# Attention and a gated feed-forward layer on one core: a store moved to another queue, and an unused path rewritten

## The chip, the core and the metric

The kernel runs on one NeuronCore of a Trainium2 chip. The core has five engines with instruction streams of their own: TensorE (PE in the profile; its weight loads are PEld), VectorE (DVE), ScalarE (ACT), GpSimd (POOL) and SyncE (SP), which computes nothing and issues transfers. A name with a q (SPq, ACTq) is the part of an engine that takes instructions in order, waits on semaphores and issues transfers. Sixteen DMA engines carry the transfers of all queues. The metric is the device time of one execution in microseconds (us), as the median of several.

## The reference

Eight batches of eight heads attend causally over 576 positions, with a decay from a cumulative sum; the result, as 4608 rows of 512, is normalized and goes through a gated feed-forward layer with 1536 inner columns.

```python
scores = 0.125 * q @ k.T                       # per head, 576 x 576, head size 64
cum    = cumsum(maximum(s, 0))
bias   = minimum(-(cum[i] - cum[j]), 0)        # causal: j <= i
attn   = softmax(scores + bias) @ v            # -> x, 4608 x 512
xn     = x / sqrt(mean(x * x) + 1e-6) * rms_g
out    = (silu(xn @ w_gate) * (xn @ w_val)) @ w_out
```

The softmax is taken with its row maximum subtracted. Inputs and output are 32-bit floats.

## The kernel before

The kernel has two paths. The **fast path** holds nearly the whole program. It leaves out the row maximum and folds the decay into factors per key, which is right only while the sums of s and the sizes of q and k stay in bounds. It runs the feed-forward layer in nine chunks of 512 rows (`ffn(c)`). Attention work for the next rows is dealt out between the matmuls of a chunk by `step()`, which looks at lists of what is due (`s_seq`, `av_seq`, `xt_seq`, `t_seq`) and at lags in slots. For each of twelve blocks of 128 inner columns, TensorE makes the gate (L946) and the value (L955), ScalarE a tanh (L949), VectorE the products (L958, L951). At the end of a chunk `store` makes four tiles of 128 output rows: twelve matmuls each (L972), a copy with factor 0.5 by ScalarE into `osb` (L976), and a transfer to `out` (L977). The last tile of the last chunk is cut into columns 0 to 383 and 384 to 511, so that its last part is short.

While that runs, VectorE gathers what the bounds need into one number, `flag_i` (L1063). After the fast path `general` begins: every engine loads `flag_i` into a register (L1269) and branches on it (L1270). If it is 0, the **general path** computes everything again by the reference's rule. It has two loops that are run by registers. The first goes over the 64 heads (L1283): loads of k, q and v by GpSimd, the cumulative sum as a row and as columns from a copy in DRAM, TensorE transposes, scores, softmax, and 64-row pieces of the result into the DRAM buffer `x_d`. The second goes over 72 tiles of 64 rows (L1366): eight loads from `x_d`, the norm, a transpose, the feed-forward layer in three parts with a transpose each, and a store. With the inputs that are timed the flag is 1 and the branch goes past all of this.

What follows at L1270 on the side that skips is made by the framework, not written in the kernel: each engine raises the semaphores that its instructions in the general path would have raised, so that later waits hold on both sides. For SyncE these are the counters of its transfers, eight of them, each with a wait for the transfers so far. Then the program ends, at the line of the launch in the profile (L1432): SyncE waits for every semaphore in turn, two at a time, twelve waits; the engines meet in a barrier that GpSimd opens; GpSimd clears the semaphores; they meet again. The program's start (L1421) has a barrier of the same kind, ahead of which SyncE sets four registers and GpSimd three.

The order of all this on each engine is that in which the code is written or dealt out (`tc.manual_schedule()`). SyncE issues the stores of L977, the DMA transposes of the fast path (L190, L495) and, in the general path, all transfers but the loads of k, q and v.

Of the kernel before, what the change touches and what calls it, by code (L numbers as in the profile page):

```python
# [9 lines left out]
BF16 = mybir.dt.bfloat16  # L10
# [16 lines left out]
def kernel(  # L27
# [12 lines left out]
    nc = tc.nc  # L40
    B, H, S, D = q.shape
# [5 lines left out]
    NSC = 5  # L47
# [888 lines left out]
    def ffn(c):  # L936

        x0 = (c * DM) % RING
        first[0], chunk[0] = slot[0], c
        Ht = mp.tile([128, FB, DM], BF16, name="Ht", tag="Ht", bufs=2)  # L940
        pend = None
        for fb in range(FB):
            fs = slice(fb * 128, (fb + 1) * 128)
            Gp = psF()
            for cc in range(CC):
                nc.tensor.matmul(Gp, lhsT=wg_sb[:, cc, fs], rhs=xnT[:, cc, x0:x0 + DM],  # L946
                                 start=(cc == 0), stop=(cc == CC - 1))
            T = mp.tile([128, DM], FP32, name="T", tag="T", bufs=2)
            nc.scalar.activation(out=T, in_=Gp, func=AF.Tanh, scale=0.5)  # L949
            if pend is not None:  # L950
                nc.vector.tensor_tensor(out=Ht[:, fb - 1, :], in0=pend[0], in1=pend[1], op=ALU.mult)  # L951
            step(tanh=True)
            Vp = psF()
            for cc in range(CC):
                nc.tensor.matmul(Vp, lhsT=wv_sb[:, cc, fs], rhs=xnT[:, cc, x0:x0 + DM],  # L955
                                 start=(cc == 0), stop=(cc == CC - 1))
            U = mp.tile([128, DM], BF16, name="U", tag="U", bufs=2)
            nc.vector.scalar_tensor_tensor(out=U, in0=T, scalar=1.0, in1=Gp,  # L958
                                           op0=ALU.add, op1=ALU.mult)
            pend = (U, Vp)  # L960
            if fb < FB - 1:
                step()
        nc.vector.tensor_tensor(out=Ht[:, FB - 1, :], in0=pend[0], in1=pend[1], op=ALU.mult)
        step()
        def store(tb, parts):

            r0 = c * DM + tb * 128
            osb = mp.tile([128, DM], FP32, name="osb", tag="osb", bufs=3)
            for p0, p1 in parts:
                Op = psF()  # L970
                for fb in range(FB):
                    nc.tensor.matmul(Op[:, p0:p1], lhsT=Ht[:, fb, tb * 128:(tb + 1) * 128],  # L972
                                     rhs=wout_sb[:, fb, p0:p1], start=(fb == 0), stop=(fb == FB - 1))
                    if fb % 4 == 3 and fb < FB - 1 and p0 == 0:
                        step()
                nc.scalar.activation(out=osb[:, p0:p1], in_=Op[:, p0:p1], func=AF.Copy, scale=0.5)  # L976
                nc.sync.dma_start(out=out[r0:r0 + 128, p0:p1], in_=osb[:, p0:p1])  # L977
            step()

        for tb in range(4):  # L980
            store(tb, [(0, 384), (384, 512)] if c == NCH - 1 and tb == 3 else [(0, DM)])
# [279 lines left out]
def general(ctx, tc, q, k, v, out, wg_sb, wv_sb, wout_sb, g_row, cum, ident_bf, flag_i):  # L1261
# [8 lines left out]
    with tc.If(flag == 0, preferred_fallthrough_block=True):  # L1270
        with tc.tile_pool(name="gd", bufs=1, space=bass.MemoryType.DRAM) as gd, \
# [3 lines left out]
            x_d = gd.tile([9 * BH + 56, 64, D], FP32, name="x_d")  # L1275
            half = gs.tile([128, 1], FP32, name="half")
            nc.vector.memset(half, -0.5)
            nc.sync.dma_start(out=cum_d, in_=cum)
            qf = q.rearrange("b h s d -> (b h) s d")
            kf = k.rearrange("b h s d -> (b h) s d")  # L1280
            vf = v.rearrange("b h s d -> (b h) s d")
# [1 line left out]
            with tc.For_i(0, BH, 1) as i:  # L1283
# [9 lines left out]
                for w, src in ((0, kf), (1, qf)):  # L1293
# [5 lines left out]
                    "o (c p) d -> p (o c) d", p=128))  # L1299
                nc.gpsimd.dma_start(out=vn[0:64, 4, 0:D], in_=vf[one, 512:576, :].rearrange(  # L1300
                    "o p d -> p (o d)"))
                nc.sync.dma_start(out=crow, in_=cum_d[one, :].to_broadcast([128, S]))
                nc.sync.dma_start(out=ccol[:, 0:4], in_=cum_d[one, 0:512].rearrange(
                    "o (c p) -> p (o c)", p=128))
                nc.sync.dma_start(out=ccol[0:64, 4:5], in_=cum_d[one, 512:576].rearrange(
                    "o p -> p o"))
                kqt = gs.tile([D, 2, 640], BF16, name="kqt")
                for w in (0, 1):
# [6 lines left out]
                for qb in range(NSC):  # L1315
                    n = rows(qb)
                    nk = qb * 128 + n
                    sp = gp.tile([128, 1024], FP32, name="sp")
                    nc.tensor.matmul(sp[0:n, 0:min(nk, 512)], lhsT=kqt[:, 1, qb * 128:qb * 128 + n],
                                     rhs=kqt[:, 0, 0:min(nk, 512)], start=True, stop=True)  # L1320
                    if nk > 512:
                        nc.tensor.matmul(sp[0:n, 512:nk], lhsT=kqt[:, 1, qb * 128:qb * 128 + n],
                                         rhs=kqt[:, 0, 512:nk], start=True, stop=True)
                    sc = gs.tile([128, 640], FP32, name="sc")
                    nc.vector.tensor_scalar(out=sc[0:n, 0:nk], in0=crow[0:n, 0:nk],
                                            scalar1=ccol[0:n, qb:qb + 1], scalar2=0.0,
                                            op0=ALU.subtract, op1=ALU.min)
                    nc.vector.scalar_tensor_tensor(out=sc[0:n, 0:nk], in0=sp[0:n, 0:nk],
                                                   scalar=0.125, in1=sc[0:n, 0:nk],
                                                   op0=ALU.mult, op1=ALU.add)  # L1330
                    nc.gpsimd.affine_select(out=sc[0:n, qb * 128:nk], in_=sc[0:n, qb * 128:nk],
                                            pattern=[[-1, n]], compare_op=ALU.is_ge,
                                            fill=-1.0e30, base=0, channel_multiplier=1)
                    mx = gs.tile([128, 1], FP32, name="mx")
                    nc.vector.tensor_reduce(out=mx[0:n], in_=sc[0:n, 0:nk], axis=AX.X, op=ALU.max,
                                            negate=True)
                    pr = gs.tile([128, 640], BF16, name="pr")
                    nc.vector.memset(pr, 0.0)
                    nc.scalar.activation(out=pr[0:n, 0:nk], in_=sc[0:n, 0:nk], func=AF.Exp,
                                         bias=mx[0:n])  # L1340
                    pq = gp.tile([128, NSC, 128], BF16, name="pq")
                    for c in range(qb + 1):
                        nc.tensor.matmul(pq[:, c, :], lhsT=pr[:, c * 128:(c + 1) * 128],
                                         rhs=ident_bf, is_transpose=True,
                                         start=(c == 0), stop=(c == qb))
                    prT = gs.tile([128, NSC, 128], BF16, name="prT")
                    nc.vector.tensor_copy(out=prT[:, 0:qb + 1, :], in_=pq[:, 0:qb + 1, :])
                    av = gp.tile([128, D + 1], FP32, name="av")
                    for c in range(qb + 1):
                        nc.tensor.matmul(av, lhsT=prT[:, c, :], rhs=vn[:, c, :],  # L1350
                                         start=(c == 0), stop=(c == qb))
                    rz = gs.tile([128, 1], FP32, name="rz")
                    nc.vector.reciprocal(out=rz[0:n], in_=av[0:n, D:D + 1])
                    xo = gs.tile([128, D], FP32, name="xo")
                    nc.vector.tensor_scalar(out=xo[0:n], in0=av[0:n, 0:D], scalar1=rz[0:n],
                                            scalar2=None, op0=ALU.mult)


                    for j in range(2 * qb, min(2 * qb + 2, 9)):
                        m = j * 64 - qb * 128  # L1360
                        nc.sync.dma_start(
                            out=x_d[bass.ds(i * 9 + 8 * j, 1)].rearrange("o p d -> p (o d)"),
                            in_=xo[m:m + 64])

            ov = out.rearrange("(t p) d -> t p d", p=64)
            with tc.For_i(0, B * 9, 1) as t:  # L1366
                xb = gs.tile([64, H, D], FP32, name="xb")
                for h in range(H):
                    nc.sync.dma_start(
                        out=xb[:, h, :],  # L1370
                        in_=x_d[bass.ds(t * 8 + 9 * h, 1)].rearrange("o p d -> p (o d)"))
                sq = gs.tile([64, H, D], FP32, name="sq")
# [7 lines left out]
                                               scalar=ssg, in1=g_row[0:64], op0=ALU.mult,  # L1380
                                               op1=ALU.mult)
                xT = gs.tile([128, CC, 64], BF16, name="xT")
                nc.sync.dma_start_transpose(out=xT, in_=xs)
                Hg = gs.tile([64, 3, DM], BF16, name="Hg")
                HT = gs.tile([128, 3, CC, 64], BF16, name="HT")
                for fc in range(3):
# [9 lines left out]
                    nc.vector.scalar_tensor_tensor(out=ug, in0=tg, scalar=1.0, in1=gv[:, 0, :],  # L1396
                                                   op0=ALU.add, op1=ALU.mult)
                    nc.vector.tensor_tensor(out=Hg[:, fc, :], in0=ug, in1=gv[:, 1, :], op=ALU.mult)
                    nc.sync.dma_start_transpose(out=HT[:, fc], in_=Hg[:, fc, :])
                og = gp.tile([64, DM], FP32, name="og")  # L1400
                for fb in range(FB):
                    nc.tensor.matmul(og, lhsT=HT[:, fb // CC, fb % CC, :], rhs=wout_sb[:, fb, :],
                                     start=(fb == 0), stop=(fb == FB - 1))
                ob = gs.tile([64, DM], FP32, name="ob")
                nc.scalar.activation(out=ob, in_=og, func=AF.Copy, scale=0.5)
                nc.sync.dma_start(out=ov[bass.ds(t, 1)].rearrange("o p d -> p (o d)"), in_=ob)


# [28 lines left out]
```

## Time and profile before

| what | us |
|---|---|
| median of three runs (357.88 to 358.39) | 358.01 |
| the profiled execution | 358.63 |
| its span, first to last instruction | 357.0 |
| TensorE busy | 344.7 (97%) |
| VectorE busy | 276.6 (77%) |
| ScalarE busy | 213.4 (60%) |
| GpSimd busy | 204.8 (57%) |

The span is cut into 40 slices of some 8.9 us. A digit is the busy share of a slice in tenths, and the clock's digits are what TensorE was granted:

```profile
PE   5989999999999999999999999999999999999993
ACT  3988785878786546864676467654665454223321
POOL 7968754457669977677697987597545400000000
PEclk9999999999999999999999999999999999999998
```

TensorE is full from the second slice on, and only the last slice drops. Times in such views count from the span's start. A row of a source line gives the count of an instruction, the shortest, median and longest duration in ns, and when the first and the last one started. A DMA instruction's duration is that of its issue; when the bytes have landed is told apart from it. Instructions that only wait or branch are not counted as busy.

### The profile page before, as it was taken

Reading aid. Unit: us, or ns where it says so; the run is one execution under the profiler, and the core shown is the slowest. Engines: PE = TensorE matmul, PEld = TensorE weight load, DVE = VectorE, ACT = ScalarE, POOL = GpSimd, SP = SyncE. Lnnn points to the kernel's source line nnn. Section 1 sums busy time; section 2 is a strip of 40 time slices with the busy share of each in tenths; the row PEclk is TensorE's granted clock in tenths of the full one; section 3 lists DMA queues with packets and bytes.
Section 4 is the critical chain, followed back from the end, with each engine's and each line's share of the span. In section 5 each row is a group of like instructions: output and inputs, shape, how many; then the busy total and the mean of one; then the engine's idle time right before and its main releaser. Section 6 shows DMA issues by size and latency. Waiting matters only on the chain.

```text
span 357.0 us, 6944 instructions
## 1 busy us (share of the span) xinstructions
PE 344.7 (97%) x2419; PEld 165.5 (46%) x2419; DVE 276.6 (77%) x524; ACT 213.4 (60%) x471; POOL 204.8 (57%) x337
## 2 busy tenths in 40 slices
PE   5989999999999999999999999999999999999993
PEld 2454444544444444544444544445444454444441
DVE  6587989598967887898889887988798579818820
ACT  3988785878786546864676467654665454223321
POOL 7968754457669977677697987597545400000000
PEclk9999999999999999999999999999999999999998
DMA  7999999999969999999899999495410221020011
GB/s 231 136 196 265 179 176 265 179 204 186 95 126 173 158 165 115 240 131 208 150 165 102 115 158 147 48 133 102 112 22 17 73 76 23 0 106 13 1 62 63
DMA packets 130528, 45.68 MB, mean 128 GB/s; under 512 B 110548, under 2 KB 125656, under 8 KB 130488
## 3 DMA queue, kind: packets, MB, share of 16 engines
q0 software_dynamic: 67056, 13.70, 49.8%
q1 hardware_dynamic: 53936, 24.26, 33.0%
q10 hardware_dynamic: 9496, 7.23, 8.2%
q8 instruction: 20, 0.33, 0.4%
q14 instruction: 20, 0.16, 0.2%
HBM read 37.90 MB, written 9.44 MB: 133 GB/s over the span
## 4 chain that ended last, share of the span: by engine, by line
PE 87%; POOL 3%; DVE 3%; issue 2%; ACT 1%; DMA 1%; SPq 0%; POOLq 0%; DVEq 0%
PE psF L972 26%; PE psF L955 23%; PE psF L946 23%; PE psS L286 2%; PE psAV L443 2%; PE psAV L437 2%; PE psF L367 2%; PE psS L367 1%; DMA kqT<-kqn 1%; POOL v_sb L409 1%; DVE x_sb L453 1%; PE psAV L1118 1%; DVE Ht L951 1%; DVE U L958 1%; PE psS L255 1%
## 5 line engine op out<-in xcount | busy, mean ns | idle before, releaser
L946 PE MATMUL psF<-xnT,wg_sb 128*128 128x512 bf16 x432 | 110.9, 379 | 0.3 <-ACT xnT L511 0.3
L955 PE MATMUL psF<-xnT,wv_sb 128*128 128x512 bf16 x432 | 111.0, 379 | 0.0
L949 ACT ACTIVATE T<-psF 128x512 f32<-128x512 f32 x108 | 64.6, 598 | 63.0 <-PE psF L946 60.9
L972 PE MATMUL psF<-wout_sb,Ht 128*128 128x512 bf16 (+2 forms) x444 | 100.9, 374 | 0.0
L958 DVE SCALAR_TENSOR_TENSOR U<-T,psF 128x512 bf16<-128x512 f32 x108 | 73.6, 682 | 24.1 <-ACT T L949 23.9
L951 DVE TENSOR_TENSOR Ht<-U,psF 128x512 bf16<-128x512 bf16 x99 | 67.8, 685 | 6.9
L972 PEld LDWEIGHTS <-Ht 128*128 128x128 bf16 x444 | 40.1, 98 | 43.5 <-issue 1.4
L955 PEld LDWEIGHTS <-wv_sb 128*128 128x128 bf16 x432 | 39.6, 98 | 44.5 <-issue 2.9
L946 PEld LDWEIGHTS <-wg_sb 128*128 128x128 bf16 x432 | 39.4, 98 | 42.9 <-issue 2.4
L976 ACT ACTIVATE osb<-psF 128x512 f32<-128x512 f32 (+2 forms) x37 | 21.7, 586 | 58.2 <-PE psF L972 51.6
L384 POOL TENSOR_SCALAR_AFFINE_SELECT E<-E 128x512 bf16<-128x512 bf16 (+1 forms) x50 | 34.8, 704 | 28.3 <-ACT E L380 18.5
L194 POOL DMA_DIRECT2D v_sb<-in_v_dram x40 | 35.2, 882 | 0.2 <-issue 0.2
L484 DVE SCALAR_TENSOR_TENSOR xs_sb<-x_sb,al_all,g_row 128x512 bf16<-128x512 bf16 (+1 forms) x36 | 29.6, 822 | 4.1 <-POOL al_all L477 3.9
L474 POOL TENSOR_SCALAR al_all<-ss_all 128x1 f32<-128x1 f32 (+2 forms) x39 | 11.5, 295 | 37.0 <-ACT xs_sb L461 29.0
L310 ACT ACTIVATE E<-psS,biasK 128x256 bf16<-128x256 f32 (+3 forms) x88 | 29.1, 425 | 2.6 <-PE psS L286 2.6
L453 DVE TENSOR_TENSOR x_sb<-psAV,rZ 128x256 bf16<-128x256 f32 (+1 forms) x66 | 28.0, 424 | 2.3
L522 DVE TENSOR_TENSOR acc<-acc,mag 128x1280 bf16<-128x1280 bf16 x32 | 27.3, 872 | 0.2
L477 POOL TENSOR_TENSOR al_all<-al_all,mhalf 128x1 f32<-128x1 f32 (+2 forms) x39 | 25.1, 645 | 3.2
L443 PEld LDWEIGHTS <-E 128*128 128x128 bf16 x320 | 21.7, 98 | 10.5 <-POOL E L384 0.7
L461 ACT ACTIVATE xs_sb<-x_sb 128x512 bf16<-128x512 bf16 (+1 forms) x37 | 23.3, 629 | 4.6 <-DVE x_sb L453 4.0
L409 POOL TENSOR_TENSOR v_sb<-v_sb,vwx 128x512 bf16<-128x512 bf16 x25 | 25.9, 1037 | 0.1
L443 PE MATMUL psAV<-v_sb,E 128*128 128x65 bf16 x264 | 23.8, 194 | 0.1
(136 smaller groups left out, 381.8 us busy)
## 6 DMA issues: line engine op xcount, KB each, us to landing
out_dram<-osb SPq DMA_DIRECT2D x35, 256.0 KB, 2.4
kq<-in_q_dram ACTq DMA_DIRECT2D x5, 1024.0 KB, 7.2
v_sb<-in_v_dram POOLq DMA_DIRECT2D x32, 128.0 KB, 5.1
kqn<-in_k_dram POOLq DMA_DIRECT2D x20, 128.0 KB, 4.8
kq<-in_k_dram SPq DMA_DIRECT2D x4, 512.0 KB, 6.0
kq<-in_q_dram SPq DMA_DIRECT2D x4, 512.0 KB, 7.6
wout_sb<-in_moe_w_out_dram POOLq DMA_DIRECT2D x2, 768.0 KB, 10.2
kq<-in_q_dram POOLq DMA_DIRECT2D x1, 1024.0 KB, 10.5
```

The costliest lines, as they stand in the source:

```text
L194: nc.gpsimd.dma_start(out=v_sb[0:n, b % 2, c, :, 0:64], in_=v[b, :, c * 128:c * 128 + n, :].rearrange("h p d -> p h d"))
L384: nc.gpsimd.affine_select(out=Ev, in_=Ev, pattern=[[0, 4], [1, nq]], compare_op=ALU.is_ge, fill=0.0, base=0, channel_multiplier=-1)
L409: nc.gpsimd.tensor_tensor(out=v_sb[:, b % 2, c, :, 0:64], in0=v_sb[:, b % 2, c, :, 0:64], in1=vwx[:, c, i:i + H].unsqueeze(2).to_broadcast ...
L443: nc.tensor.matmul(o, lhsT=d, rhs=v_sb[:, p, qb, h, :], start=(j == 0 and qb == 0), stop=(j == 3))
L453: nc.vector.tensor_tensor(out=xo[:, g * 256:(g + 1) * 256].rearrange("p (h d) -> p h d", h=4), in0=pv[R, :, 0:64], in1=rZ[R].unsqueeze(2). ...
L484: nc.vector.scalar_tensor_tensor(out=xs_sb[R, (b * NSC + qb) % NX, :], in0=x_sb[R, (b * NSC + qb) % NX, :], scalar=al_all[R, col:col + 1], ...
L946: nc.tensor.matmul(Gp, lhsT=wg_sb[:, cc, fs], rhs=xnT[:, cc, x0:x0 + DM], start=(cc == 0), stop=(cc == CC - 1))
L949: nc.scalar.activation(out=T, in_=Gp, func=AF.Tanh, scale=0.5)
L951: nc.vector.tensor_tensor(out=Ht[:, fb - 1, :], in0=pend[0], in1=pend[1], op=ALU.mult)
L955: nc.tensor.matmul(Vp, lhsT=wv_sb[:, cc, fs], rhs=xnT[:, cc, x0:x0 + DM], start=(cc == 0), stop=(cc == CC - 1))
L958: nc.vector.scalar_tensor_tensor(out=U, in0=T, scalar=1.0, in1=Gp, op0=ALU.add, op1=ALU.mult)
L972: nc.tensor.matmul(Op[:, p0:p1], lhsT=Ht[:, fb, tb * 128:(tb + 1) * 128], rhs=wout_sb[:, fb, p0:p1], start=(fb == 0), stop=(fb == FB - 1))
```

## The change

The store of the very last 128 columns is issued from ScalarE's queue, where its copy out of PSUM is made, in place of SyncE's. In the general path, each transfer that SyncE issued is issued by GpSimd, and the four DMA transposes of a tile become four small TensorE transposes each, into PSUM, with a copy back by VectorE (`turn`).

```diff
                 nc.scalar.activation(out=osb[:, p0:p1], in_=Op[:, p0:p1], func=AF.Copy, scale=0.5)
-                nc.sync.dma_start(out=out[r0:r0 + 128, p0:p1], in_=osb[:, p0:p1])
+                (nc.scalar if p0 else nc.sync).dma_start(out=out[r0:r0 + 128, p0:p1], in_=osb[:, p0:p1])
...
-            nc.sync.dma_start(out=cum_d, in_=cum)
+            nc.gpsimd.dma_start(out=cum_d, in_=cum)
...
-                nc.sync.dma_start(out=crow, in_=cum_d[one, :].to_broadcast([128, S]))
+                nc.gpsimd.dma_start(out=crow, in_=cum_d[one, :].to_broadcast([128, S]))
...
-                        nc.sync.dma_start(
+                        nc.gpsimd.dma_start(
                             out=x_d[bass.ds(i * 9 + 8 * j, 1)].rearrange("o p d -> p (o d)"),
                             in_=xo[m:m + 64])
+
+            def turn(dst, src):
+                px = gp.tile([128, NSC, 128], BF16, name="pq")
+                for c in range(CC):
+                    nc.tensor.matmul(px[:, c, 0:64], lhsT=src[:, c * 128:(c + 1) * 128],
+                                     rhs=ident_bf[0:64, 0:64], is_transpose=True,
+                                     start=(c == 0), stop=(c == CC - 1))
+                nc.vector.tensor_copy(out=dst, in_=px[:, 0:CC, 0:64])
...
-                nc.sync.dma_start_transpose(out=xT, in_=xs)
+                turn(xT, xs)
...
-                    nc.sync.dma_start_transpose(out=HT[:, fc], in_=Hg[:, fc, :])
+                    turn(HT[:, fc], Hg[:, fc, :])
...
-                nc.sync.dma_start(out=ov[bass.ds(t, 1)].rearrange("o p d -> p (o d)"), in_=ob)
+                nc.gpsimd.dma_start(out=ov[bass.ds(t, 1)].rearrange("o p d -> p (o d)"), in_=ob)
```

On ScalarE, at the end of the fast path, this is a piece of the difference between the two built programs (a row is the line, the instruction, what it writes and reads, and the shape; lines that begin with + are new):

```order
 L976 ACTIVATE osb<-psF 128x384
 L976 ACTIVATE osb<-psF 128x128
+L977 DMA out_dram<-osb 128x128
 L1269 TENSOR_LOAD flag_i
 L1270 COMPARE_AND_BRANCH
 L1283 COMPARE_AND_BRANCH
 L1283 UNCONDITIONAL_BRANCH x2
```

The store now stands between ScalarE's last copy and its load of the flag, and ScalarE's branch behind both.

On SyncE, at the same place and on into the general path (`cum_d` and `crow` are the cumulative sum in DRAM and as a row):

```order
 L977 DMA out_dram<-osb 128x512 x3
 L977 DMA out_dram<-osb 128x384
-L977 DMA out_dram<-osb 128x128
 L1270 COMPARE_AND_BRANCH
-L1278 DMA cum_d<-cum 64x576
 L1283 COMPARE_AND_BRANCH
 L1283 UNCONDITIONAL_BRANCH x2
-L1432 BRANCH_PREFETCH_HINT
-L1283 ISA
-L1302 DMA crow<-cum_d 128x576
```

SyncE's branch now follows the store of 384 columns directly, and of its general path only the loops' branches stay. Its 182 rows become 136; GpSimd's 342 become 390. Ahead of the branch nothing else on any engine differs but the registers set at the start: SyncE's four are gone, and GpSimd sets two more.

More of the change, by code (lines that the diff above doesn't have):

```diff
@@ L1301, in general @@
                     "o p d -> p (o d)"))
[L1302 to L1303 removed]
+                nc.gpsimd.dma_start(out=crow, in_=cum_d[one, :].to_broadcast([128, S]))
+                nc.gpsimd.dma_start(out=ccol[:, 0:4], in_=cum_d[one, 0:512].rearrange(
                     "o (c p) -> p (o c)", p=128))
[L1305 removed]
+                nc.gpsimd.dma_start(out=ccol[0:64, 4:5], in_=cum_d[one, 512:576].rearrange(
                     "o p -> p o"))
@@ L1368, in general @@
                 for h in range(H):
-                    nc.sync.dma_start(
+                    nc.gpsimd.dma_start(
                         out=xb[:, h, :],
```

## The prediction

> **What bounds the kernel now.** I read the page first: its busy shares and the chain that ended last.
>
> ```profile
> span 357.0 us, 6944 instructions
> PE 344.7 (97%) x2419; PEld 165.5 (46%) x2419; DVE 276.6 (77%) x524; ACT 213.4 (60%) x471; POOL 204.8 (57%) x337
> PE 87%; POOL 3%; DVE 3%; issue 2%; ACT 1%; DMA 1%; SPq 0%; POOLq 0%; DVEq 0%
> ```
>
> TensorE is busy for 97% of the span and makes 87% of the chain. The change gives it, on the path that is run, nothing more and nothing less. So the stages are not where this is decided; next I cut the span at the end of the arithmetic.
>
> ```profile
> 351.20:357.00 5.80, 0.00 (x0) 0.00 (x0) 0.00 (x0) 0.00 (x0) 0.00 (x0) 0.80 0.15 49
> ```
>
> This row (stretch, its length, then busy time of PE, PEld, DVE, ACT, POOL) says that 5.8 us at the end hold no arithmetic at all. It is this tail that the change edits, so I went through it by source line: the stores (L977), the branch (L1270), the end of the program (L1432).
>
> ```profile
> 350.86 0.28 ACT L976 ACTIVATE osb<-psF 128x128 f32<-128x128 f32 x1
> 350.76 1.53 SPq L977 DMA_DIRECT2D out_dram<-osb  x2
> L977 SPq DMA_DIRECT2D out_dram<-osb x2: 332/718/1103, 350.8 to 351.2; - x2
> out_dram<-osb SPq DMA_DIRECT2D x1, 192.0 KB, 2.5
> out_dram<-osb SPq DMA_DIRECT2D x1, 64.0 KB, 2.9
> L1270 SPq COMPARE_BRANCH  x1: 58/58/58, 352.3 to 352.3; - x1
> L1270 SPq EVENT_SEMAPHORE  x3: 17/17/17, 352.9 to 353.1; - x3
> L1270 SPq EVENT_SEMAPHORE  x5: 17/17/17, 355.0 to 355.3; - x5
> SPq L1270 <- SPq L1270: 2.4, 2, 1.9
> L1432 SPq EVENT_SEMAPHORE  x10: 28/28/28, 355.4 to 356.0; - x10
> L1432 SPq EVENT_SEMAPHORE  x4: 17/22/28, 356.0 to 357.0; - x4
> L1432 POOLq EVENT_SEMAPHORE  x4: 17/17/17, 356.2 to 356.9; - x4
> ```
>
> In a line's row stand the count, the shortest, median and longest duration in ns, and the first and last start; in a store's row its KB and the us from issue to landing. ScalarE copies the last 128 columns out by 350.86 + 0.28 = 351.14. SyncE issues their store at 351.2, right behind that of the 384 columns; the one issue takes 332 ns, the other 1103, so SyncE is free at 350.76 + 1.53 = 352.29. The bytes have landed at 351.2 + 2.9 = 354.1. SyncE doesn't see that: it branches at 352.3, does three of eight small steps, stands still until 355.0 (the row of waits gives the longest gap as 1.9 us and names SyncE itself), does the other five, and only from 355.4 walks through the twelve waits that end the program. Ten of these start between 355.4 and 356.0; the eleventh, at 356.0, is the one that asks for the last store. Then the barrier through GpSimd (356.2 to 356.9) and the end at 357.0. So **SyncE's own sequence bounds the tail**: the end comes 357.0 - 354.1 = 2.9 us after the last byte, of which 357.0 - 356.0 = 1.0 is needed behind the wait for it.
>
> **The change part by part.**
>
> *The general path.* Not one row of the trace stands on its lines (L1278 to L1406), so none of its transfers, transposes or copies is run, and their direct cost is nothing, with no cover needed. What it costs is at the skip. The eight steps at L1270 bring SyncE's eight DMA counters to the values that SyncE's transfers in the general path would have left; with no transfer of SyncE there, all eight go, and GpSimd's counters are raised instead. GpSimd does its share early:
>
> ```profile
> L1270 POOLq COMPARE_BRANCH  x1: 45/45/45, 336.9 to 336.9; - x1
> L1270 POOLq EVENT_SEMAPHORE  x4: 17/30/43, 337.4 to 337.7; - x4
> L1432 POOLq DRAIN  x3: 46/107/1052, 338.2 to 356.8; - x3
> L1270 ACTq COMPARE_BRANCH  x1: 54/54/54, 351.4 to 351.4; - x1
> L1270 ACTq EVENT_SEMAPHORE  x1: 17/17/17, 351.9 to 351.9; - x1
> q14 instruction: 1, 0.01, 4.0%
> ```
>
> GpSimd branches at 336.9, is at the program's end by 338.2 and is next needed at 356.2: a fifth such step there, and even a standstill as long as SyncE's, lie under the last matmuls. If that cover were gone they would cost 0.1 and 1.9 us.
>
> The standstill of 1.9 us is the larger thing. In 353.2 to 354.0, inside it, the queue named instruction moves one piece (last row), so I take it for a fetch of SyncE's code. GpSimd and ScalarE branch over the same path and go on 0.5 us later (336.9 to 337.4, 351.4 to 351.9) without a standstill. In the built program SyncE's branch passes 166 of its instructions before the change and 68 after; GpSimd passes 96 and ScalarE 79 before. At 68 SyncE is below both engines that don't stand still, so I take the standstill as gone; bounds: 0 and 1.9 us.
>
> *The store's queue.* ScalarE issues it in its own order, ahead of its load of the flag and its branch. SyncE branches when the 384-column issue is over, 350.76 + 0.33 = 351.1 in place of 352.3, so 1.2 us earlier. Without a standstill it goes on at 351.6 and stands at its eleventh wait by 351.6 + 0.6 = 352.2, well ahead of any landing. Hence after the change the end is the landing + 0.05 (a step's pace is (356.0 - 355.4) / 10 = 0.06) + 1.0, rounded to 1.1, against 2.9: **-1.8 us**.
>
> The landing itself has no row for a store from ScalarE's queue. Its bounds:
>
> ```profile
> L977 SPq DMA_DIRECT2D out_dram<-osb x3: 332/332/337, 343.7 to 348.9; - x3
> DMA to landing us min/median/max: 2.0/2.0/2.0
> L137 ACTq DMA_DIRECT2D kq<-in_q_dram x5: 372/382/385, 71.3 to 159.9; - x5
> q8 instruction: 1, 0.02, 5.4%
> out_dram<-osb SPq DMA_DIRECT2D x1, 256.0 KB, 3.7
> ```
>
> Three undisturbed stores from SyncE land after 2.0 us each: the low end. The high end is the 2.9 of this very store on SyncE's queue, 1103 - 332 = 771 ns of which is a slow issue: another piece of instructions was being moved in 350.9 to 352.0 (fourth row; from the queue of the larger pieces, right after TensorE's branch). ScalarE's issues take 372 to 385 ns, so without the slow issue this store would land after 2.9 - 0.77 = 2.1; but the same fetch is still there, and the 384 columns that met it needed 2.5. The store at 312.3, which met one as well, needed 3.7 (last row). I take 2.3, between 2.1 and 2.5: 351.2 + 2.3 = 353.5 for 354.1, **-0.6 us** (from -0.9 to 0).
>
> Queued behind the issue on ScalarE are its load of the flag, its branch, one step and its entry into the barrier:
>
> ```profile
> L1269 ACTq TENSOR_LOAD <-flag_i x1: 488/488/488, 350.9 to 350.9; - x1
> L1432 ACTq DRAIN x2: 8/8/8, 352.0 to 356.5; - x2
> L1421 SPq MOVE  x4: 29/34/42, 0.0 to 0.2; - x4
> L1421 POOLq MOVE  x3: 29/29/39, 0.1 to 0.3; - x3
> ```
>
> The load ran beside the last copy, at 350.9, and the first entry was at 352.0: 1.1 us. Now it starts behind the issue, at 351.2 + 0.4 = 351.6, and the entry comes at 352.7, before the landing at 353.5. It costs nothing; with an issue of 1.1 us it would be 353.4, still covered.
>
> *The start.* Four register moves leave SyncE and two are added to GpSimd (counted in the built programs). GpSimd is the engine that opens the start barrier: two moves of 0.03 us each by their duration, of 0.07 by the pace of SyncE's four (0.2 / 3), so 0.06 to 0.14, **+0.1 us** on everything.
>
> **The sum**: -1.8 - 0.6 + 0.1 = -2.3 us. The profiled execution took 358.63 us, its span 357.0 and 1.6 around it that the change leaves alone; the median of the runs shown is 358.01, 0.6 lower, and the difference is laid on that: 358.0 - 2.3 = **355.7**. With the landing from 2.0 to 2.9 us this case gives 355.4 to 356.3.
>
> **The rivals.**
>
> *The standstill stays, or the whole tail merely moves up.* Whether SyncE's code is at hand after the branch isn't shown by any row for the new distance; of the three engines above, one stood still. Then SyncE resumes 355.0 - 352.3 = 2.7 us after a branch at 351.1, at 353.8, and runs twelve waits and the barrier (357.0 - 355.4 = 1.6): 355.4 + 0.1 for 357.0, so -1.5 and 356.5. Least of all comes off where everything behind SyncE's branch takes as long as before and only starts 1.2 us earlier: -1.2 + 0.1, which is 356.9. Against the first, the two shorter branches; against the second, the eight steps, which have no counter left to raise.
>
> [...]
>
> *The store from ScalarE's queue lands late, and the kernel is slower.* The only rows of that queue are loads:
>
> ```profile
> kq<-in_q_dram ACTq DMA_DIRECT2D x5, 128.0 KB, 5.7
> ```
>
> With 5.7 us the landing is at 356.9 and the end 1.1 later, 358.0 + 0.1 for 357.0: +1.1, and 359.1. It decides from a landing of 4.7 us on (351.2 + 4.7 + 1.1 + 0.1 = 357.1). Against it: those loads ran among other traffic, while in the tail the DMA share is 0.15.
>
> *The change does not do what it says for the time*: something besides SyncE ends the program, say GpSimd after its longer jump, and only the start's +0.1 is left, 358.1. Against it: GpSimd is at the program's end from 338.2 on.
>
> **How the numbers follow.** The likeliest case has 0.75: every step of it has a row but the landing and the distance of the branch. The standstill gets 0.09, the tail merely moved up 0.04, the late landing 0.05, no effect 0.07. A measurement of this kernel can tell about 0.2%, 0.7 us, from no change. The first three are faster by more than that (356.9 is 1.1 below 358.0): faster 0.88, same 0.07, slower 0.05. The range goes from 354.9, half a microsecond under the likeliest case's own low end, as the landing of 64 KB may come sooner than that of the three stores of 256 KB, to 356.9, the tail moved up; it leaves out the last two cases.
>
> **What would show it.** In the profile after: SyncE's branch near 351.2, no eight steps at L1270, a gap under 0.6 us behind it, and the twelve waits begun before 352; the last wait released by the landing, which is 2.0 to 2.9 us after the issue at 351.3; the end 1.1 us after that landing, near 354.7. The span up to the last copy longer by 0.1. The prediction is wrong if SyncE still stands still behind its branch, if the landing from ScalarE takes over 3 us, or if ScalarE or GpSimd enters the barrier after SyncE.

## The result, and the profile after

The changed kernel takes 356.04 us in the median of seven runs (355.54 to 357.23); the kernel before, beside it on the same chip, 358.39 (357.88 to 359.27). The ratio is 0.9939, with a 95% interval of 0.9923 to 0.9955: 0.6% or 2.2 us faster. The prediction was 355.7, faster, with a range of 354.9 to 356.9.

The profiled execution took 355.58 us. Its page begins:

```profile
span 354.1 us, 6889 instructions
PE 340.6 (96%) x2374; PEld 165.3 (47%) x2419; DVE 276.9 (78%) x524; ACT 213.4 (60%) x471; POOL 204.5 (58%) x337
```

Some TensorE records are missing there (2374 for 2419), so its busy time is not to be compared. The cut behind the last copy is (stretch, length, busy times, granted clock, DMA share, GB/s):

```profile
350.45:354.10 3.65, 0.00 (x0) 0.00 (x0) 0.00 (x0) 0.00 (x0) 0.00 (x0) 0.87 0.23 76
```

3.65 us without arithmetic stand where 5.8 stood (5.9 when they too are counted from the last copy's end). By source line, on SyncE and ScalarE:

```profile
L1270 SPq COMPARE_BRANCH  x1: 58/58/58, 350.4 to 350.4; - x1
L1440 SPq EVENT_SEMAPHORE  x9: 28/28/46, 351.0 to 351.5; - x9
L1440 SPq EVENT_SEMAPHORE  x1: 28/28/28, 352.7 to 352.7; - x1
L1440 SPq EVENT_SEMAPHORE  x4: 17/22/28, 353.1 to 354.0; - x4
L977 ACTq DMA_DIRECT2D out_dram<-osb x1: 379/379/379, 350.5 to 350.5; - x1
L1440 ACTq DRAIN  x2: 8/8/8, 352.1 to 353.5; - x2
```

(L1440 is now the line of the program's end; in the kernels further down it is L1432 to L1442, as their edits move it.) SyncE branches at 350.4, has no step at L1270, and is in its waits from 351.0. Nine run through; the tenth goes at 352.7, when the 384 columns have landed, the eleventh at 353.1, when the last 128 have. The end follows at 354.1. ScalarE enters the barrier at 352.1, ahead of all that. From issue to landing both parts take 2.6 us:

```profile
out_dram<-osb SPq DMA_DIRECT2D x1, 192.0 KB, 2.6
out_dram<-osb ACTq DMA_DIRECT2D x1, 64.0 KB, 2.6
```

The standstill has moved to GpSimd, whose jump got longer:

```profile
L1270 POOLq COMPARE_BRANCH  x1: 45/45/45, 336.2 to 336.2; - x1
L1270 POOLq EVENT_SEMAPHORE  x5: 17/43/43, 338.9 to 339.2; - x5
```

It now goes on 2.7 us after its branch, in place of 0.5. GpSimd is next needed at 353.3, so this costs nothing.

The two profiled executions differ by 3.05 us, more than the runs do. The first load of SyncE starts 0.10 us later than before (of the two rows below, the first is before, the second after), and yet the last copy ends at 350.45 in place of 351.14. I put those 0.8 us down to scatter: in eight further kernels with the same work up to there the last copy ends between 350.72 and 351.57, and in a ninth (e6) at 352.71, in an execution of 357.12 us where that kernel's others took 354.6 to 355.1. In what follows I therefore compare the **stretch**, from the last copy's end to the end of the span.

```profile
0.93 0.47 SPq L137 DMA_DIRECT2D kq<-in_k_dram  x1
```

```profile
1.03 0.46 SPq L137 DMA_DIRECT2D kq<-in_k_dram  x1
```

### The profile page after: what moved, and what is told of

Read it like the earlier page. It is cut to its first block, busy times and chain, and to the rows that moved or that the text cites. A ratio compares the mean times of both kernels' runs of the same rounds, so it can differ in the third digit from the quotient of the medians.

```text
span 354.1 us, 6889 instructions
## 1 busy us (share of the span) xinstructions
PE 340.6 (96%) x2374; PEld 165.3 (47%) x2419; DVE 276.9 (78%) x524; ACT 213.4 (60%) x471; POOL 204.5 (58%) x337
## 4 chain that ended last, share of the span: by engine, by line
PE 77%; DVE 8%; POOL 4%; issue 4%; DMA 3%; ACT 2%; SPq 0%; DVEq 0%; POOLq 0%; ACTq 0%
PE psF L972 25%; PE psF L955 21%; PE psF L946 20%; DVE U L958 2%; PE psAV L443 2%; DMA kq<-in_q_dram 2%; DMA kqT<-kqn 2%; PE psS L286 2%; DVE Ht L951 1%; PE psAV L437 1%; DVE x_sb L453 1%; PE psF L367 1%; POOL v_sb L409 1%; POOL v_sb L194 1%; PE psS L367 1%
## 5 line engine op out<-in xcount | busy, mean ns | idle before, releaser
L955 PE MATMUL psF<-xnT,wv_sb 128*128 128x512 bf16 x424 | 109.9, 379 | 0.4
L946 PE MATMUL psF<-xnT,wg_sb 128*128 128x512 bf16 x414 | 109.0, 379 | 1.3 <-ACT xnT L511 0.3
L972 PE MATMUL psF<-wout_sb,Ht 128*128 128x512 bf16 (+2 forms) x428 | 98.9, 373 | 1.4 <-issue 0.8
```

## The experiments

This table has every kernel that ran; times are medians, landings are counted in us from the last copy's end, and the ratio is to the kernel before on the same chip.

| kernel | us | ratio (95%) | stretch | 384 columns landed | last 128 landed | end after that |
|---|---|---|---|---|---|---|
| before | 358.39 | 1 | 5.90 | 2.11 | 2.91 | 2.99 |
| changed | 356.04 | 0.9939 (0.9923 to 0.9955) | 3.64 | 2.22 | 2.60 | 1.04 |
| e1, store alone | 357.50 | 0.9965 (0.9950 to 0.9980) | 4.73 | 2.36 | 2.53 | 2.20 |
| e2, path alone | 356.38 | 0.9942 (0.9919 to 0.9964) | 3.95 | 2.45 | 2.91 | 1.04 |
| e3, long jump | 357.15 | 0.9957 (0.9940 to 0.9974) | 4.56 | 2.61 | 2.78 | 1.78 |
| e4, eight steps, short jump | 357.27 | 0.9965 (0.9949 to 0.9981) | 4.64 | 2.33 | 2.85 | 1.80 |
| e5, short path, ScalarE | 356.11 | 0.9933 (0.9920 to 0.9946) | 3.67 | 1.51 | 2.63 | 1.04 |
| e6, no path | 355.02 | 0.9898 (0.9884 to 0.9913) | 2.70 | 1.50 | 1.71 | 0.99 |
| e7, changed again | 356.11 | 0.9938 (0.9922 to 0.9953) | 3.68 | 2.39 | 2.64 | 1.04 |
| e8, short path, SyncE | 355.41 | 0.9908 (0.9894 to 0.9923) | 2.76 | 1.51 | 1.72 | 1.04 |
| e9, path alone, 6 idle matmuls | 357.68 | 0.9970 (0.9958 to 0.9983) | 5.01 | 3.80 | 3.97 | 1.04 |
| e10, path alone again | 356.25 | 0.9927 (0.9913 to 0.9941) | 3.85 | 2.38 | 2.80 | 1.04 |
| e11, changed, 6 idle matmuls | 357.73 | 0.9971 (0.9959 to 0.9983) | 4.52 | 3.30 | 3.48 | 1.04 |
| e12, path alone, 10 idle matmuls | 357.32 | 0.9957 (0.9944 to 0.9970) | 4.63 | 1.64 | 3.59 | 1.04 |

e1 to e4, e5 to e8 and e9 to e11 ran together on one chip each; the kernel before took 358.69, 358.51 and 358.93 there, and 358.75 beside e12.

### What SyncE's skip costs: e1 to e4

My theory (A) was that two separate things go: the standstill, which hangs on where the jump lands in SyncE's code, and the steps themselves, with the wait that they hold. Its rivals were that the steps as such stand still (B), and that the queue of the last store is all that matters (C).

**The store alone.** The kernel before, with the new line for the store and nothing else.

```diff
-                nc.sync.dma_start(out=out[r0:r0 + 128, p0:p1], in_=osb[:, p0:p1])
+                (nc.scalar if p0 else nc.sync).dma_start(out=out[r0:r0 + 128, p0:p1], in_=osb[:, p0:p1])
```

> The kernel before with only the last 128 columns' store moved to ScalarE's queue; the general path as it was. Theory A (SyncE's code is fetched in pieces, and the skip lands shortly ahead of a piece's edge): SyncE's branch comes 1.2 us earlier, against the end of the last copy, and as two of SyncE's instructions ahead of the edge are gone, it does five of the eight steps, not three, and then stands still until 2.6 to 2.7 us after its branch. The eight steps and twelve waits follow, and the kernel is 1.2 us faster than before (0.9 to 1.5). Theory B (the fourth step waits for something of the transfers, not for code): three steps again, standstill until about 0.9 us after the last landing, 1.0 us faster. Theory C (all of the gain is the queue of the store): 2.3 us faster.

```profile
L1270 SPq COMPARE_BRANCH  x1: 58/58/58, 351.3 to 351.3; - x1
L1270 SPq EVENT_SEMAPHORE  x5: 17/17/17, 351.8 to 352.2; - x5
L1270 SPq EVENT_SEMAPHORE  x3: 17/17/17, 354.1 to 354.3; - x3
L1432 SPq EVENT_SEMAPHORE  x11: 27/28/28, 354.4 to 355.0; - x11
```

1.2 us faster. SyncE branches right behind the 384 columns' issue, takes five steps, stands still from 352.2 to 354.1, takes three more, and is in its waits at 354.4, after the landing at 351.30 + 2.53 = 353.83. Before the change three steps came ahead of the standstill and five behind it. In this kernel SyncE has two instructions fewer ahead of its branch, so a standstill behind two steps more lies at the same place of SyncE's code, as theory A has it. The sixth step, though, asks for the store of the 384 columns, which landed at 351.30 + 2.36 = 353.66: until then SyncE would have waited here in any case, and only the 0.5 us from there to 354.1 can't be that wait. In the kernel before there is no such doubt: the fourth step asked for a store that had landed at 348.3, and SyncE stood ahead of it until 355.0.

**The path alone.** The changed kernel with the store back on SyncE's queue; e10 is the same kernel on another chip.

```diff
-                (nc.scalar if p0 else nc.sync).dma_start(out=out[r0:r0 + 128, p0:p1], in_=osb[:, p0:p1])
+                nc.sync.dma_start(out=out[r0:r0 + 128, p0:p1], in_=osb[:, p0:p1])
```

> The changed kernel with the store of the last 128 columns back on SyncE's queue; only the general path is rewritten. Theory A: the issue of the last store takes 1.1 us again, SyncE branches 1.2 us after the last copy, has no step to do and does not stand still, so it is at its waits before the landing, which comes 2.9 us after the issue as before; the end is 1.1 us behind it, and the kernel is 1.7 us faster than before (1.4 to 2.3). Theory B (the steps themselves are what waits): the same, 1.7 us. Theory C: no gain.

> The kernel with only the general path rewritten, again, beside the other two on one chip: 2.1 us below the kernel before (1.7 to 2.4), SyncE's second issue 1.1 to 1.5 us long, the stretch from the last copy's end to the end 3.8 to 4.0 us.

```profile
L977 SPq DMA_DIRECT2D out_dram<-osb x2: 332/886/1441, 350.3 to 350.8; - x2
L1270 SPq COMPARE_BRANCH  x1: 58/58/58, 352.3 to 352.3; - x1
L1440 SPq EVENT_SEMAPHORE  x10: 27/28/28, 352.8 to 353.4; - x10
L1440 SPq EVENT_SEMAPHORE  x4: 17/22/28, 353.6 to 354.6; - x4
out_dram<-osb SPq DMA_DIRECT2D x1, 64.0 KB, 2.9
```

The ratio is 0.9942 here and 0.9927 in e10 (2.6 us, where I had expected at most 2.4); that of the whole change is 0.9939 and 0.9938. So **the rewritten path alone brings what can be measured of the gain**, although SyncE's second issue is as slow as ever (1441 ns) and its branch as late. SyncE reaches its eleventh wait by 353.4, 0.2 us ahead of the landing, and that is enough. The two parts don't add up (1.2 and 2.1 against 2.2 together), since each brings SyncE to its last waits earlier, and once it stands there ahead of the landing, as with the path alone, more of that gains nothing.

**A long jump with nothing in it to do.** The changed kernel with 160 instructions of SyncE in the path that is not run, so that its branch passes 229 in place of 68.

```diff
+            for _ in range(160):
+                nc.sync.drain()
             nc.gpsimd.dma_start(out=cum_d, in_=cum)
```

> The changed kernel with 160 drain instructions for SyncE put into the general path, which is not run; SyncE's branch then passes 229 instructions in place of 68, still with no step to do. Theory A: SyncE stands still for 2.1 to 2.7 us right behind its branch, before the first of the twelve waits; from the branch at 0.0 it goes on at 2.6, the waits and the barrier take 1.65, so the kernel is 0.7 us slower than the changed one (0.4 to 1.5) and 1.6 us faster than before. Theory B: no standstill, as fast as the changed kernel.

```profile
L1270 SPq COMPARE_BRANCH  x1: 58/58/58, 351.1 to 351.1; - x1
L1442 SPq EVENT_SEMAPHORE  x12: 27/28/28, 354.0 to 354.7; - x12
```

The standstill is back: 2.9 us from the branch to the first wait, in place of 0.5, with no step at L1270 at all. That is against B.

**Eight steps after a short jump.** The path alone, with one transfer of the path split in eight and given back to SyncE; its branch passes 76 instructions.

```diff
-            nc.gpsimd.dma_start(out=cum_d, in_=cum)
+            for i in range(8):
+                nc.sync.dma_start(out=cum_d[i * 8:i * 8 + 8], in_=cum[i * 8:i * 8 + 8])
```

> As the kernel with only the general path rewritten, but there SyncE issues the copy of the cumulative sum, in eight pieces, so that eight counters have to be raised on the side that skips, while its branch passes 76 instructions. Theory A: no standstill; the eight steps run at 0.09 us each until the one that asks for the last store, which waits for its landing; then one more step and twelve waits at 0.06 us, and the end comes 1.8 us after the landing in place of 2.9: 1.1 us faster than before (0.8 to 1.6). Theory B: the standstill of 1.9 us at the fourth step is back, and the kernel is within 0.4 us of before.

```profile
L1270 SPq EVENT_SEMAPHORE  x6: 17/17/17, 352.9 to 353.3; - x6
L1270 SPq EVENT_SEMAPHORE  x2: 17/17/17, 353.8 to 353.8; - x2
L1441 SPq EVENT_SEMAPHORE  x14: 17/28/28, 353.9 to 355.5; - x14
```

Six steps run through without a standstill. The seventh holds until the last store has landed (350.92 + 2.85 = 353.76), and the twelve waits come behind it: the end is 1.80 us after the landing in place of 1.04. So the steps cost 0.8 us even without a standstill, because one of them asks for the last store ahead of the waits. C falls with e2, which gains 2.1 us on SyncE's queue. B falls with e3, which stands still with no step to do, and with e4, where steps run without a standstill.

### Why the last store lands late: e5 to e8

The landing was my mis-sized term: 2.57 us after the issue, where I had 2.3. The trace reports a store's landing in 16 parts. In the changed kernel 14 or 15 of the 16 land 1.5 to 1.9 us after the issue, for either store, and one or two 0.7 to 0.9 later. Theory F: these wait behind a piece of instructions that is moved as TensorE branches (16 KB; 350.29 to 351.22 in the changed kernel's profile). Theory T: the last stores are late in any case.

**A short path, the store from either queue.** e5 is the changed kernel with the inner loops of the path cut to one pass each, e8 the same with the store on SyncE's queue.

```diff
-                for qb in range(NSC):
+                for qb in range(1):
...
-                for fc in range(3):
+                for fc in range(1):
...
-                for fb in range(FB):
+                for fb in range(1):
```

> The changed kernel with the unused general path cut to one pass of each of its inner loops (one block of rows, one part of the feed-forward layer, one matmul where there were four or twelve). For these inputs the path is not run and the output is the same; for inputs that need it, most of its computation is left out. TensorE's branch now passes 81 of its instructions in place of 257, SyncE's 68 as before. Theory F (the last part of the last store waits behind the piece of 16 KB of instructions that is moved as TensorE branches): no such piece is moved in the last 5 us, both parts of the last tile land 2.0 to 2.1 us after their issue in place of 2.6, the end is 1.0 after the later landing, the stretch from the last copy's end to the program's end is 3.0 to 3.2 us in place of 3.6: 0.5 us faster than the changed kernel on the same chip (0.3 to 0.7). Theory T (the last part is late because two stores of the same tile follow each other within 0.4 us, or because the chip's last write is always confirmed late): landing 2.5 to 2.6 us after the issue as before, same time as the changed kernel to 0.2 us.

> As the kernel with the short general path (most of the path's computation is left out), but with the last 128 columns stored from SyncE's queue as before the change. Theory F (SyncE's slow issue of 1.1 to 1.4 us is made by the same moved piece of instructions): the issue takes 0.33 us, the store lands 2.0 to 2.1 us after an issue that stands at the same place, SyncE reaches its waits 1.5 us before the landing, and the time is that of the short path with ScalarE's store to 0.2 us: the store's queue is then worth nothing. Rival (two issues of SyncE within 0.1 us of each other are slow in themselves): the issue takes 1.1 us or more again, landing 2.5 to 2.9 after it began, 0.5 to 0.9 us slower than with ScalarE's store.

**No path.** e6 leaves out the call of `general`, e7 is the changed kernel beside them.

```diff
-    general(ctx, tc, q, k, v, out, wg_sb, wv_sb, wout_sb, g_row, cum, ident_bf, flag_i)
```

> The changed kernel without the general path, its load of the flag and its branches; the path that needs them is left out, and for these inputs the output is the same. Theory F: no engine jumps, so no piece of instructions is moved by a jump in the tail, the last store lands 2.0 to 2.1 us after its issue, the wait for it is the last to end, and the stretch from the last copy's end to the end is 3.0 to 3.2 us in place of 3.6; 0.5 us faster than the changed kernel (0.3 to 0.8), 2.8 faster than the kernel before. Theory T: landing still 2.5 to 2.6 after the issue, and the same time as the changed kernel to 0.2 us. By both, what the branch itself still costs in the changed kernel is nothing, since SyncE waits for the landing there too.

> The changed kernel itself, beside the others on one chip: 2.2 us below the kernel before (1.8 to 2.6), the last store landing 2.4 to 2.8 us after its issue, and the stretch from the last copy's end to the end 3.5 to 3.8 us.

The rows of the queues from 349.9 us on, and the landings (q8 moves instructions in pieces of 16 KB, q14 in pieces of 8 KB, and q10 the store from ScalarE's queue), first of e7:

```profile
q8 instruction: 1, 0.02, 1.0%
q14 instruction: 2, 0.02, 0.9%
out_dram<-osb SPq DMA_DIRECT2D x1, 192.0 KB, 2.8
out_dram<-osb ACTq DMA_DIRECT2D x1, 64.0 KB, 2.6
```

then of e5, followed by two short cuts out of it (352.8 to 353.4 and 353.3 to 353.7):

```profile
q14 instruction: 2, 0.02, 1.1%
out_dram<-osb SPq DMA_DIRECT2D x1, 192.0 KB, 1.9
out_dram<-osb ACTq DMA_DIRECT2D x1, 64.0 KB, 2.6
...
q14 instruction: 1, 0.01, 5.3%
q10 hardware_dynamic: 24, 0.01, 5.1%
...
q10 hardware_dynamic: 9, 0.00, 3.5%
```

of e8:

```profile
L977 SPq DMA_DIRECT2D out_dram<-osb x2: 332/358/383, 351.0 to 351.4; - x2
q14 instruction: 2, 0.02, 1.2%
out_dram<-osb SPq DMA_DIRECT2D x1, 192.0 KB, 1.9
out_dram<-osb SPq DMA_DIRECT2D x1, 64.0 KB, 1.7
```

and the last landing of e6, which has no row of instructions:

```profile
out_dram<-osb ACTq DMA_DIRECT2D x1, 64.0 KB, 1.7
```

In e5, e6 and e8 the 16 KB piece (q8) is gone, and the 384 columns land after 1.9 us with all their parts close together: T falls for them. In e6 and e8 the last 128 land after 1.7. That is 0.9 us less than in the changed kernel, twice what I had expected, and the kernels are 1.1 and 0.7 us faster than e7. SyncE's second issue takes 383 ns in e8, so it was the 16 KB piece that made it 1.1 to 1.4 us, not the nearness of two issues.

But e5 is a miss: with ScalarE's store the last 128 still need 2.6 us, and the kernel is no faster than e7. A piece of 8 KB (q14) is moved from 352.86 to 353.37, and nine of the store's 144 packets, one part of sixteen, move only behind it (the last row: 9 packets, in 353.3 to 353.7). This piece begins 1.3 us after SyncE's branch. In the changed kernel, e7 and e11 a piece begins 1.3 to 1.5 us after SyncE's branch too, so I take it for SyncE's; it was not tried by itself. The changed kernel's own packets show it at work too: of its two late parts of the last store, the one that lands last begins to move at 352.23, where a piece of 8 KB (351.72 to 352.23) ends, and the other at 352.09, behind the late part of the 384 columns. That fits a landing that stayed at 2.6 when the 16 KB piece alone was gone. With the store on SyncE's queue, SyncE branches only behind the store's issue (351.8 in e8); the first piece then begins 1.53 us behind the last copy's end, in place of 1.29 in e5, and misses the store. So **in the kernel with the short path, the store on ScalarE's queue is 0.7 us slower than on SyncE's** (356.11, lowest 355.98, against 355.41, highest 355.61). It isn't the queue as such: in e6, where nothing branches, ScalarE's store lands after 1.7 us.

### The piece moved in time: e9, e11, e12

If a late piece is the cause, delaying TensorE's branch should move the piece behind the stores, in a complete kernel. Six or ten matmuls that nobody reads stand behind the last useful one, in e9 and e12 with the store on SyncE's queue, in e11 on ScalarE's.

```diff
-            ffn(c)
+            ffn(c); c == NCH - 1 and warm(6)
```

> The kernel with only the general path rewritten (the last store on SyncE's queue), complete, and with six matmuls of 128 by 512 whose result nobody reads on TensorE behind its last useful one, so that TensorE's branch comes 1.3 us later (six times 0.216). Theory F (a piece of instructions that a branch brings in holds back a part of the store that it meets): the piece of 16 KB begins some 1.3 us after the last copy's end and no longer meets the stores, whose bytes are under way up to 1.1 us after that end; SyncE's second issue takes 0.33 to 0.38 us in place of 1.1 to 1.4, the store lands 1.7 to 2.0 us after it, and the stretch from the last copy's end to the end is 2.7 to 2.8 us in place of 3.9 of the same kernel without the six: 0.9 us faster than that kernel (0.6 to 1.2) and 0.7 faster than the changed kernel, 3.1 below the kernel before. TensorE is at the barrier 0.5 us or more before it is asked for. Rival (the unused path's length costs in another way): the stretch stays at 3.5 us or more.

> The changed kernel, complete, with the same six matmuls behind TensorE's last useful one. Theory F with SyncE's own piece: SyncE branches right behind the 384 columns' issue here, its piece of 8 KB begins 1.05 to 1.5 us after that branch, while the bytes of ScalarE's store are under way, and one of the store's parts is late as with the short general path; the 384 columns land in 1.9 to 2.0 us, the last 128 in 2.4 to 2.7, the stretch from the last copy's end to the end is 3.5 to 3.7 us: the same time as the changed kernel to 0.3 us, and 0.7 us slower than the same six matmuls with the store on SyncE's queue. Rival (only TensorE's piece matters): landing 1.7 to 2.0 us after the issue, the stretch 2.7 to 2.9 us, 0.7 to 0.9 faster than the changed kernel.

> As the kernel with six idle matmuls and the store on SyncE's queue (complete), with ten in place of six. There TensorE's branch came 0.53 us ahead of the last copy's end and its piece 0.56 us behind that end, into the stores' bytes. Four more matmuls of 0.216 us put the branch 0.86 later and the piece at 1.4 us behind the copy's end. Theory F: the stores' bytes are under way up to 1.1 us behind that end, so no part is late: the last store lands 1.7 to 2.0 us after its issue, TensorE reaches the barrier about 2.0 us behind the copy's end (0.1 later than the others), and the stretch from the copy's end to the end is 2.7 to 2.9 us: 355.6 to 356.0 where the kernel before has 358.5 to 358.9, 0.5 to 0.9 faster than the rewritten path without idle matmuls and 1.8 to 2.2 faster than with six. Rival (idle matmuls themselves slow the end, by TensorE's later arrival): slower than with six by the 0.9 us that four more take, 358.5.

TensorE's branch, the idle matmuls and SyncE's stores in e9 by source line, then the queue of the piece and the landings:

```profile
L1270 PEldq COMPARE_BRANCH  x1: 358/358/358, 350.7 to 350.7; - x1
L849 PE MATMUL psF<-mneg,ident_bf x6: 379/380/380, 350.8 to 351.8; 128*128 128x512 bf16 x6
L977 SPq DMA_DIRECT2D out_dram<-osb x2: 332/358/383, 350.9 to 351.3; - x2
q8 instruction: 1, 0.02, 2.0%
out_dram<-osb SPq DMA_DIRECT2D x1, 192.0 KB, 4.2
out_dram<-osb SPq DMA_DIRECT2D x1, 64.0 KB, 3.9
```

All three missed on the time: e9 is 1.4 us slower than e10 beside it; by their ratios e11 is 1.2 us slower than the changed kernel and e12 1.1 slower than e10. e9's piece began 0.56 us behind the last copy's end, at 351.80, in the midst of the stores' bytes, and took 1.91 us; one part of each store landed 2.3 us after the other fifteen (355.04 and 355.21 against 352.55 to 352.94). In e11 parts are late by up to 1.8 us in the same way. The piece that meets the stores in full thus costs more than the one that only meets their beginning, which bears theory F out, though not my means of escaping it. My working failed in that TensorE's branch does not wait for its matmuls: in e9 it is taken at 350.7, and the last idle matmul starts at 351.8 (last start of the second row). Ten idle matmuls put the branch only 0.22 us later against the last copy's end than six. The piece begins within 0.1 us of the last idle matmul's start in all three (351.80 and 351.8 in e9, 351.47 and 351.5 in e11, 352.50 and 352.4 in e12).

In e12 the piece began at 352.50, later than every byte of 15 of the 16 parts of the last store, and still its last part came behind the piece (two cuts, 352.4 to 353.4 and 353.4 to 354.0, and the landing):

```profile
DMA packets 3, 0.03 MB, mean 33 GB/s; under 512 B 0, under 2 KB 0, under 8 KB 0
q14 instruction: 2, 0.02, 6.8%
q8 instruction: 1, 0.02, 6.1%
...
DMA packets 9, 0.00 MB, mean 7 GB/s; under 512 B 1, under 2 KB 9, under 8 KB 9
out_dram<-osb SPq DMA_DIRECT2D x1, 64.0 KB, 3.5
```

From 352.4 to 353.4 only three pieces of instructions move; the nine packets of the last part move after 353.4. So the moment at which a piece's record begins does not tell whether a store's part comes behind it. What does, and where TensorE's branch would have to stand for the piece to miss the stores, stays open. No complete kernel that ran beats the changed one by more than the noise; e8 shows what there would be to gain, 0.7 us.

## Why the prediction was right, step by step

- **What bounds the tail.** Right. SyncE's sequence did, and the end now follows the landing by 1.04 us, where I had 1.1.
- **SyncE's part, -1.8 us.** Right in its mechanism: 2.99 - 1.04 = 1.95 in the profiles. The two reasons that I gave for it, the standstill and the eight steps with the later branch, are each shown alone by e3 and e4, where the end again comes 1.78 and 1.80 us after the landing: each alone costs some 0.75. That SyncE's standstill hangs on what its branch passes is shown by e3: 2.9 us from the branch to the first wait with 229 instructions passed, 0.5 to 0.6 with 68 (e2 and the changed kernel). My reason for it, the distance, is not: e1's branch passes the same code as the kernel before's, and its standstill came behind five steps in place of three, which speaks for a place in the code (with the doubt named there). That 68 instructions came out on the good side was in part luck. In e3 the standstill follows the branch directly; in the kernel before and in e1 three and five steps run first. What decides where it comes, no run here shows. Which piece in the trace ends which standstill could not be settled: in e3 it ended 0.3 us behind one, in the kernel before 1.1.
- **The landing, -0.6 us.** This term was mis-sized. Against the last copy's end the landing came 2.91 - 2.60 = 0.31 us earlier, since it took 2.57 us from the issue and not 2.3. I had seen the 16 KB piece beside the stores and allowed 0.2 us for it; by e6, where no piece is moved, the pieces cost this store 0.9 (2.6 against 1.7). The piece of 8 KB had no term at all. My 2.1 without the slow issue was misread for the same reason: in the kernel before, 15 of the last store's 16 parts had landed 2.2 to 2.3 us after the issue began, and the last one, at 2.87, began to move at 353.13, where a piece of 8 KB (352.60 to 353.13) ends. What the change does avoid is SyncE's slow issue. Nor can the 0.3 be told in the time: the path alone, without it, is as fast within the noise.
- **The start, +0.1 us.** Right, by SyncE's first load (0.93 to 1.03). That the span up to the last copy grows by as much can't be seen under 0.8 us of scatter.
- **The sum.** -1.95 - 0.31 + 0.10 = -2.16, where -2.3 was forecast: SyncE's part was 0.15 too small and the landing's 0.3 too large, and the two errors partly cancel; the ratio's interval, 0.9923 to 0.9955, is -2.8 to -1.6.
- **What was costed at nothing.** GpSimd did stand still, 2.7 us, and its cover held. ScalarE entered the barrier at 352.1, 0.9 us ahead of the landing.
- **The rivals.** What I had worked out for a standstill that stays (-1.5 us) is what e3 measured (-1.5, 357.15 for 358.69), and the tail merely moved up (-1.1) is e1 (-1.2): right as sums, but neither happened here. The landing of 5.7 us did not come; but that the move to ScalarE can cost time is shown by e5 against e8 (356.11 against 355.41 us), by another mechanism than the one I named. That ScalarE issued the last store in 0.38 us, where SyncE took 1.44 in e2, left nothing in the time that these runs can tell.

## What to carry to other kernels

Code that is never run can cost time at the end of a program: by what its skip makes an engine do (semaphores brought up, one of them held by the last store: 0.8 us in e4), by what the jump passes (2.9 us to the first wait in e3 in place of 0.5), and by the piece of instructions that is moved at the jump while the last stores are under way (the last one landed after 2.6 us in e7, and after 1.7 in e6, where no piece was moved). Read the tail by engine and line from the last arithmetic on, and ask of each engine whether it stands at its last wait ahead of the last landing; once it does, further time saved there is worth nothing, and two edits that both bring it there don't add up (here 1.2 and 2.1 us alone, 2.2 together). Where a store lands late, look at its parts, 16 here: one or two late parts beside a piece of instructions say more than the mean.

## What the runs showed of the hardware that I had not expected

- In several tails a late part of a store begins to move just as a piece of instructions ends (e5: both at 353.37; before: both at 353.13; e12: 353.44 and 353.47). Why, no view here shows. A piece took from 0.4 us (8 KB, before: 355.65 to 356.05) to 1.9 us (16 KB, e9), and a late part landed up to 2.3 us after the others (e9). Without a late part 64 KB landed 1.7 us after the issue (e6, e8).
- An issue of SyncE took 1.1 to 1.4 us while TensorE's piece was being moved (1.10 before, 1.44 in e2) and 0.38 us when the piece was gone or began later (e8, e9, e12); ScalarE's took 0.38 us beside the same piece (the changed kernel).
- TensorE's branch runs ahead of its matmuls: in e9 it was taken at 350.7, with the last matmul started at 351.8. Its own duration was 354 to 364 ns where a piece of 16 KB was moved, and 229 ns in e5 and e8, where none was.
- GpSimd, too, went on only 2.7 us after its branch in the changed kernel, whose jump is longer, where it had taken 0.5 in the kernel before.
